# Linear attention's products in 64x64 quarters of TensorE, ahead of a mixture of experts

## The chip, the core and the metric

The kernel runs on one core of one Trainium2 chip. The metric is the device time of one execution in microseconds (us). A core has a matrix engine (TensorE, PE in the profile), a vector engine (VectorE, DVE), an activation engine (ScalarE, ACT), a general engine (GpSimd, POOL) and a queue engine (SyncE, SP). DMA transfers bring data from memory; here they are issued mostly by POOL and SP. TensorE multiplies a stationary block, loaded by a weight load (PEld), with a stream of columns, and writes to PSUM, from where VectorE and ScalarE read.

## What is computed

```python
def phi(x): return np.where(x > 0, x, np.exp(x) - 1.0) + 1.0
q_p, k_p = phi(q), phi(k)                      # (8, 8, 576, 64): batch, head, token, feature
kv  = np.einsum('bhsd,bhse->bhde', k_p, v)
z   = np.sum(k_p, axis=2)
num = np.einsum('bhsd,bhde->bhse', q_p, kv)
den = np.einsum('bhsd,bhd->bhs', q_p, z)[..., None] + 1e-06
x   = (num / den).transpose(0, 2, 1, 3).reshape(4608, 512)
P   = np.exp(x @ w_gate - max)                 # 8 experts
for _ in range(8):                             # sinkhorn: rows, then columns
    P /= P.sum(1, keepdims=True) + 1e-09
    P /= P.sum(0, keepdims=True) + 1e-09
    P *= 4608 / 8
out = sum(P[:, e:e+1] * (np.maximum(x @ w1[e], 0) @ w2[e]) for e in range(8))   # w1 512x1024, w2 1024x512
```

## The kernel before, in words

The program has two parts. The **front** is the attention of 16 items (8 batches times 2 groups of four heads), and it fills the tile xT with x, features on partitions, in fp16. The rest is the experts: layer 1 (x times w1, relu), layer 2 (times w2, scaled by P and added up), in blocks of 512 tokens, most of them by a scheme that multiplies 7 blocks in place of 8 (block7 and unit). While the front runs, the first blocks of expert 0 are worked off between its steps (hq at line 684, ye at line 932), so that TensorE has something to do.

**The order.** Every step is recorded in a planner (class _Plan) as a task with an engine, an assumed duration, a priority, and the buffers that it takes and uses. For the front the order is not planned: the string _FRONT lists task numbers with a letter for the engine (p TensorE, a ScalarE, d VectorE, g GpSimd, s SyncE, m a DMA, n none), and run() issues them just so. Once the list is used up, the planner picks by its assumed times and priorities. It also has a constant TURN, 0.13, that it adds on TensorE when a task's field cfg differs from that of the task ahead; before, cfg=1 marks only the kv task.

**One item,** in att(b, g), has four heads in two pairs; hh (0, 1) is the head inside a pair, which is also the half of the 128 partitions (64 partitions with 9 tokens each), and r (0, 1) is the pair:
- k (fp32), q and v (cast to fp16) are loaded by a DMA each (line 380). v goes into two of three blocks of a tile vv whose middle block holds ones.
- exp(k) on ScalarE (L390), max(k+1, 1) on VectorE (L394) and the minimum of both (L398) give phi(k), tile t. q goes the same way (L447, L450, L454), tile tq.
- f_kv (L413): 9 token steps times 2 halves hh, contraction over 64 partitions. The stationary block is 64x128, the heads of both pairs side by side, and the streamed one is v0, ones, v1: 192 columns. Of the result only the blocks that belong together are wanted.
- f_z (L340 on ScalarE, L342 on VectorE): two copies of 64 partitions by 256 columns put kv and z into the tile kvz, in which the off-diagonal blocks stay zero. Those zeros are set once by two memsets on GpSimd ahead of all loads (L604).
- f_qt (L439): 9 transposes of 128x128 turn phi(q), one copy (L342 or L340) brings it to SBUF, tile qpT.
- heads (L470): with the 128x128 block of kvz as stationary, two matmuls of 288 columns each give den (tile att) or num (tile num_ps) for half the tokens. So there are four such groups an item: den and num for each half.
- ScalarE takes the logarithm of den (L483) and exp of its negative (L488); VectorE multiplies num with that into xT (L498).

The zeros in kvz let one 128-row matmul do two heads at once, and half of its products are with zeros. After every second batch nine token blocks of logits are computed (L515, 36 matmuls of 8 columns), and after the last the sinkhorn loop starts (lines 541 to 565, its column sums by a matmul at L556). 46 warm-up matmuls (L590) fill TensorE's time at the start.

The order of the 512 features of x within xT is free as long as w1 (load_w1, L315) and the router weights (f_wg, L585) are loaded in the same order.

Of the kernel before, what the change touches and what calls it, by code (L numbers as in the profile page):

```python
# [11 lines left out]
FP16 = mybir.dt.float16  # L12
# [5 lines left out]
class _Plan:  # L18
# [121 lines left out]
    48s 49m 1n 2p 3p 52g 53m 4p 50g 51m 5p 6p 78g 79m 7p 8p 76g 77m 9p 10p 126g 127m 54a 55d 11p 12p 80g 81m 13p 14p  # L140
    128g 129m 56d 108n 109g 110m 57n 58p 0g 15p 130g 131m 16p 17p 18p 19p 20p 21p 61n 62a 63d 154g 155m 22p 23p 24p 25p
    26p 59a 64d 27p 111g 112m 60a 28p 29p 89n 90a 30p 91d 65p 31p 66d 32p 82a 156g 157m 33p 83d 67p 34p 68a 84d 158g
    159m 132a 69p 92d 35p 36p 133d 85n 86p 114g 115m 70a 71a 93p 87d 116g 117m 37p 88d 38p 94d 139n 140a 72p 39p 73d
    95p 40p 182g 183m 96a 134d 74p 75d 97p 41p 98a 184g 185m 141d 135n 136p 142d 99a 42p 143p 161d 186g 187m 137a 43p
    138a 144d 44p 160a 102p 210g 211m 145p 103d 113n 602p 146a 45p 162d 46p 47p 100p 119n 167n 120g 168a 169d 121m 603p
    101d 147p 148a 170d 163n 164p 212g 213m 149a 171p 165d 604p 214g 215m 166a 172d 152p 153d 173p 605p 174a 240g 241m
    555d 118n 606p 150p 601n 607a 175p 151d 608p 176a 610p 242g 243m 609d 188a 612p 189d 614p 244g 245m 195n 196a 190d
    616p 197d 613a 611d 191n 123g 192p 124m 615a 198d 618p 193a 194a 106g 217d 107m 177a 180p 199p 617d 216a 620p 181d
    200d 178p 619a 270g 271m 179d 621a 201p 122n 624p 202a 223n 225d 268g 269m 224a 639p 218d 203p 562d 638n 640a 219n
    220p 300g 301m 204a 226d 622p 205a 221d 298g 299m 222d 227p 247d 206p 228a 641p 207d 104g 105m 643p 253n 255d 246a  # L150
    642d 272g 273m 229p 644d 208p 230a 645p 209d 254a 231p 248d 647p 232a 256d 326g 327m 249n 250p 233a 646d 302g 303m
    257p 251d 125n 623p 252a 258d 281n 282a 236p 283d 259p 237d 625p 260a 284d 234p 632a 649p 235d 274a 261p 275d 628p
    262a 276d 354g 355m 629p 648a 311n 313d 563g 263a 285p 266p 286d 651p 304a 328g 329m 267d 238p 330g 331m 650a 630d
    356g 357m 277n 278p 305d 239a 306d 626p 279a 280a 333d 312a 264p 287p 265d 627p 288a 384g 385m 652d 307n 308p 332a
    314d 440g 441m 289p 309d 634a 653p 382g 383m 636d 290a 310d 358g 359m 672p 556d 291a 334d 315p 292p 654a 316d 659p
    339n 340a 293d 317p 657p 361d 318a 360a 341d 294p 660p 295d 319p 557d 412g 413m 671n 673d 335n 336p 320a 558s 559m
    442g 443m 342d 658p 337a 321a 338d 343p 667d 322p 367n 368a 344d 674p 323d 296p 388a 362d 324p 297a 369d 655p 675a
    325d 414g 415m 665a 345p 395n 397d 656p 386g 387m 346a 370d 416g 417m 396a 676p 389d 564d 347p 418a 390d 363n 364p
    565s 566m 567s 568m 348a 661p 365d 444g 445m 398d 677a 371p 349a 366d 662p 372d 663a 352p 373p 353d 678p 374a 425n
    427d 350p 679a 375p 351d 680p 376a 419d 426a 391n 392p 420d 669a 399p 500g 501m 428d 377a 688p 576g 393d 400d 682p  # L160
    394a 446a 681d 380p 401p 381d 690p 402a 498g 499m 447d 683a 378p 684p 379d 496g 497m 403p 577d 685d 421n 422p 404a
    448d 429p 423a 472g 473m 424a 686p 430d 405a 583g 406p 687d 705p 453n 454a 407d 431p 691p 455d 432a 468g 469m 510n
    512d 511a 408p 584g 433p 409d 707p 434a 698d 470g 471m 449n 450p 704n 708a 456d 505g 706d 689p 451a 435a 513d 457p
    709p 696a 458d 452a 502a 692p 578d 475d 579s 580m 438p 560s 561m 459p 439d 694p 460a 581s 582m 436p 461p 437d 711p
    462a 481n 483d 464p 463a 503d 410p 693p 465d 411a 712a 504d 482a 514p 466p 695p 467d 474a 710d 506n 507p 515a 484d
    713p 476d 508a 509a 715p 741d 714a 702d 516p 742d 477n 478p 517a 569d 716a 518p 727p 479d 519a 570g 480a 485p 520a
    521p 486d 717p 522d 487p 719p 718d 488a 571d 523p 720a 489p 700d 572s 573m 746p 490a 574s 575m 524d 748p 491a 743d
    494p 721p 745n 747a 495d 749a 728p 744d 585d 492p 750p 493d 752p 553n 784d 751a 785d 525p 753a 737d 754p 786d 526a
    787s 788m 528d 756p 586s 587m 755a 789s 790m 735a 722p 757a 738d 554p 588s 589m 729a 527n 529p 723p 739d 530d 1015s
    1016m 724p 740d 531d 758p 760p 759a 725p 761a 762d 792p 532p 794p 793a 590g 533d 597n 598g 599m 726p 763d 795a 731a  # L170
    591n 592g 593m 796p 764d 733a 798p 534d 842g 800p 799a 766p 802p 767a 806p 791n 797a 768p 801d 807a 803d 535p 770p
    536d 843d 808p 537d 844g 812p 809a 772p 813a 771a 814p 773a 816p 804p 769a 817d 776p 845s 846m 805a 765d 1072s
    1073m 810p 777d 818p 815d 774p 819a 900d 811a 850p 538p 820d 901g 778p 851a 775d 856p 779a 539d 864p 857a 594g 595m
    902d 866p 821d 854p 824p 540d 849n 855a 860p 825a 826p 865a 867a 852p 870p 822d 853a 872p 871a 861d 830p 873d 874p
    831a 868p 875d 862p 596n 1007d 834p 863a 823d 827a 876p 1008d 869a 541p 858p 835d 908p 958g 832p 859d 909a 877a
    836p 833d 542d 912p 837a 878d 910p 922p 959d 911a 879d 914p 828p 543d 915a 882p 907n 913a 829a 916p 923a 918p 883a
    924p 917d 928p 925a 1009d 884p 929a 919d 888p 880d 885a 960d 930p 889a 881d 961s 962m 544p 932p 903s 904m 926p 933d
    963s 964m 892p 927a 931d 920p 893d 905s 906m 934p 921a 545d 890p 546d 847s 848m 966p 968p 967a 886p 935a 969a 894p
    891d 547p 972p 936d 895a 980p 887a 937d 970p 940p 548d 965n 971a 549d 973a 942p 981a 941a 974p 976p 986p 975d 984p
    946p 977d 985a 943a 938d 550p 944p 947a 551d 987a 552d 982p 950p 983a 939d 637g 783a 990p 951d 978p 991d 988p 979a  # L180
    948p 1010d 1018p 949d 992p 1019a 989d 1020p 635a 952p 1024p 600n 1006n 1011d 1021a 1000p 953a 1025a 1026p 957g 631a
    1022p 1028p 993a 701g 998p 1017n 1029d 1023a 1027d 1001p 699g 1030p 1005d 1032p 1528n 1529g 1530m 1012d 1034p 1033a
    996p 1013d 898g 703a 999p 1035a 1038p 1004a 839g 1040p 1031a 1036p 1039a 997p 633g 1037a 1041d 1042p 1075p 1043d
    994p 1076a 1003d 1077p 1014d 1044p 1078a 945d 995p 1129s 1130m 1045a 1081p 1046d 1002a 1083p 1047d 1079p 1050p
    1048d 1049d 1052p 1051a 1082a 1055p 1054d 730d 1085p 1053d 1058a 1060p 1074n 1080a 1086d 1059g 668a 1063p 666g
    1061d 1084d 1087p 1062d 1089p 780g 1088a 1065d 1091p 1090a 1066p 1092a 664g 1056a 1095p 1068d 1097p 1064d 1096a
    896g 1093p 1067d 1099p 670d 1094a 1132p 840g 1134p 1133a 1100d 1069p 1135a 1098d 1101p 1070d 1138p 1071d 1102a
    1186s 1187m 1140p 1139a 1103d 1136p 1107p 1131n 1137a 1104d 1109p 1105d 1108a 736a 1106d 1112p 1111d 1110d 1142p
    1113a 1117p 1115a 1143d 1114g 1120p 1116g 1119d 897d 1144p 955g 1118d 1146p 1145a 1148p 1147a 1123p 841g 1149a
    1152p 1125d 1154p 1124d 1534n 1535g 1536m 1153a 1150p 1141d 732a 1156p 1057g 1189p 1151a 1157d 1191p 1190a 1121d  # L190
    1126p 1192a 1155d 697a 1158p 1122d 1195p 1128d 1159a 1243s 1244m 1127d 1197p 1196a 1160d 1193p 1164p 1161d 1166p
    1162d 1165a 781a 1169p 1168d 1188n 1194a 1167d 1199p 1163d 1174p 1200d 1177p 1175d 1176d 1201p 1198d 1203p 1205p
    1204a 1180p 1206a 1202a 1209p 1182d 1211p 1181d 1210a 1207p 1170a 1213p 1208a 1246p 1214d 1248p 1247a 1212d 1183p
    1249a 1178d 1172a 1215p 1185d 1252p 1184d 1216a 1300s 1301m 1254p 1217d 1250p 1221p 1179d 1245n 1251a 1218d 1223p
    1222a 1219d 1253a 1226p 1220d 734a 1224d 1256p 1227a 1225d 1231p 1257d 1228g 1234p 1171g 1232d 1255d 1258p 1173g
    1233d 1260p 782d 954g 1262p 1261a 1237p 1263a 1259a 1266p 1531g 1532m 1239d 1268p 1238d 1267a 1264p 1235d 838a
# [28 lines left out]
def kernel(  # L225
# [10 lines left out]
    nc = tc.nc  # L236
# [125 lines left out]
    def att(b, g):  # L362
# [70 lines left out]
        def qps():  # L433
            return (at2.rearrange("p a b -> p (a b)").bitcast(FP16)[:, 0:NJ * P]
                    .rearrange("p (j h w) -> p h j w", h=2, w=PW))
# [167 lines left out]
    for t in kvz_t:  # L603
        nc.gpsimd.memset(t, 0.0)  # L604
# [604 lines left out]
```

## Time and profile before

| what | us |
|---|---|
| median of 3 runs (964.11 to 965.62) | 964.44 |
| the profiled execution | 967.64 |
| its span in the trace | 965.6 |
| TensorE, VectorE, ScalarE, GpSimd busy | 950.3, 782.0, 579.3, 184.6 |
| the last multiply into xT ends | 118.9 |
| the last logits' exponential starts | 120.7 |

Busy times of TensorE count each matmul from its start to its modelled end, so that matmuls overlap; what one costs is the distance to the next start. In a timeline row stand the start, the duration of the merged group, the engine, the line, what it writes and reads, the array's tile (rows*columns) and the streamed shape, and the count; in brackets the idle time ahead and what ended it. "issue" means that the profile shows nothing that was waited for.

### The profile page before, as it was taken

The page shows a single profiled execution, that of the slowest core. Times are in us where ns is not written, and L with a number is a line of the kernel's source. Part 1 is how long each engine was busy: PE and PEld are TensorE (multiplying, and loading weights), DVE is VectorE, ACT ScalarE, POOL GpSimd, SP SyncE. Part 2 cuts the span into 40 slices and gives each one's busy share as a digit, 9 for nine tenths or more (in the row PEclk, how much of TensorE's full clock was granted, in tenths as well). Part 3 has the DMA queues.
Part 4 walks back from the last instruction along what each step waited for, and adds up shares of the span by engine and source line. Part 5 has one row for each costly group of instructions (what it writes and reads, how often), then busy time and mean ns, then how long its engine had stood idle before and what let it go on. Part 6 is the DMA issues. An engine that isn't in the chain of part 4 may idle for free.

```text
span 965.6 us, 21108 instructions
## 1 busy us (share of the span) xinstructions
PE 950.3 (98%) x8576; PEld 805.2 (83%) x8576; DVE 782.0 (81%) x1474; ACT 579.3 (60%) x1031; POOL 184.6 (19%) x238
## 2 busy tenths in 40 slices
PE   7999999999999999999999999999999999999998
PEld 4555568888888888888888888888888888888886
DVE  6899899778888788878887888878887888877775
ACT  6898856666655555555555555555555555555553
POOL 6435021452111121111112111111112111111110
PEclk9999999999999999999999999999999999999999
DMA  9999382225323352262226322272226322235654
GB/s 220 244 249 209 106 235 80 53 88 121 98 77 100 99 120 78 89 153 78 77 78 133 105 72 72 72 159 71 76 75 139 100 77 77 78 99 164 165 163 111
DMA packets 45681, 112.52 MB, mean 117 GB/s; under 512 B 4368, under 2 KB 25616, under 8 KB 45584
## 3 DMA queue, kind: packets, MB, share of 16 engines
q1 hardware_dynamic: 21056, 75.57, 24.0%
q0 software_dynamic: 24128, 35.07, 19.8%
q8 instruction: 67, 1.10, 0.5%
q10 hardware_dynamic: 400, 0.52, 0.2%
q14 instruction: 30, 0.25, 0.1%
HBM read 119.69 MB, written 17.69 MB: 142 GB/s over the span
## 4 chain that ended last, share of the span: by engine, by line
PE 95%; DMA 2%; DVE 2%; issue 0%; ACT 0%; POOL 0%; DVEq 0%; ACTq 0%; POOLq 0%
PE ye L1050 36%; PE hq L810 24%; PE R L810 12%; PE Zye L810 6%; PE Zye L1050 6%; PE ye L932 4%; PE hq L684 3%; DMA vv<-in_v_dram 2%; PE kv_ps L413 1%; PE att L439 1%; PE att L470 1%; PE num_ps L470 1%; DVE wt L549 0%; PE att L515 0%; PE yw L590 0%
## 5 line engine op out<-in xcount | busy, mean ns | idle before, releaser
L1081 DVE SCALAR_TENSOR_TENSOR acc<-ye,P_sb,acc 128x256 f32<-128x256 f32 x620 | 268.8, 479 | 124.7 <-PE ye L1050 123.1
L810 PEld LDWEIGHTS <-W 128*128 128x128 f16 x2144 | 209.9, 98 | 25.5
L1050 PEld LDWEIGHTS <-S 128*128 128x128 f16 x1984 | 194.1, 98 | 22.8 <-DVE S L1021 0.4
L1091 POOL TENSOR_TENSOR acc<-acc,st 128x256 f32<-128x256 f32 x124 | 88.1, 730 | 601.0 <-ACT st L1088 594.5
L1050 PE MATMUL ye<-T,S 128*128 128x256 f16 x1488 | 192.8, 273 | 0.1
L810 PEld LDWEIGHTS <-w 128*128 128x128 f16 x1608 | 157.5, 98 | 19.8 <-issue 1.1
L1050 PEld LDWEIGHTS <-h 128*128 128x128 f16 x1584 | 154.9, 98 | 18.0
L845 ACT ACTIVATE h<-hq 128x512 f16<-128x512 f32 x134 | 80.2, 598 | 130.6 <-PE hq L810 127.7
L810 PE MATMUL R<-xs,W 128*128 128x256 f16 x1008 | 151.2, 273 | 0.0
L810 PE MATMUL hq<-xs,W 128*128 128x256 f16 x1008 | 151.2, 273 | 0.0
L810 PE MATMUL hq<-xs,w 128*128 128x256 f16 x1008 | 140.9, 273 | 0.3 <-DVE h L848 0.3
L825 ACT COPY Zye<-hq 128x512 f32<-128x512 f32 x134 | 77.7, 580 | 47.6 <-PE hq L810 47.3
L842 ACT ACTIVATE h<-Zye 128x512 f16<-128x512 f32 x134 | 80.0, 597 | 43.0 <-PE Zye L810 42.7
L848 DVE CUSTOM_DVE_ANT_0 h<-R,s 128x512 f16<-128x512 f32 x126 | 86.5, 686 | 13.0 <-ACT s L832 13.0
L1021 DVE TENSOR_TENSOR S<-h 128x1024 f16<-128x1024 f16 x124 | 86.1, 694 | 11.2 <-ACT h L845 11.2
L1088 ACT ACTIVATE st<-Zye,P_sb 128x256 f32<-128x256 f32 x124 | 53.1, 471 | 69.1 <-PE Zye L1050 68.2
L832 ACT COPY s<-hq 128x512 f32<-128x512 f32 x126 | 73.5, 583 | 32.3 <-PE hq L810 31.8
L848 DVE CUSTOM_DVE_ANT_0 h<-hq,s 128x512 f16<-128x512 f32 x126 | 86.6, 687 | 5.1 <-PE hq L810 2.6
L810 PE MATMUL Zye<-xs,w 128*128 128x256 f16 x504 | 75.6, 273 | 0.0
L839 ACT COPY s<-R 128x512 f32<-128x512 f32 x126 | 74.6, 592 | 1.2 <-PE R L810 0.7
L1050 PE MATMUL ye<-w,h 128*128 128x256 f16 x528 | 68.4, 273 | 0.0
L1050 PE MATMUL Zye<-w,h 128*128 128x256 f16 x528 | 68.4, 272 | 0.0
(125 smaller groups left out, 1013.8 us busy)
## 6 DMA issues: line engine op xcount, KB each, us to landing
xs<-xd SPq DMA_DIRECT2D x63, 896.0 KB, 4.6
kin<-in_k_dram POOLq DMA_DIRECT2D x15, 576.0 KB, 8.3
out_dram<-acc SPq DMA_DIRECT2D x67, 128.0 KB, 2.4
w<-in_moe_w_dram POOLq DMA_DIRECT2D x16, 512.0 KB, 7.7
w<-in_moe_w_dram POOLq DMA_DIRECT2D x7, 1024.0 KB, 13.1
vv<-in_v_dram POOLq DMA_DIRECT2D x16, 288.0 KB, 9.0
qin<-in_q_dram POOLq DMA_DIRECT2D x16, 288.0 KB, 7.6
xd<-acc SPq DMA_DIRECT2D x5, 512.0 KB, 3.6
```

The lines of the kernel that those rows point to most:

```text
L810: nc.tensor.matmul(dst[:, p, :], lhsT=lhs(p, c), rhs=rhs(c), start=(first and p == 0 and c == 0), stop=(c == 1), skip_group_check=True)
L825: nc.scalar.copy(out=Zt[1], in_=gX["tile"])
L832: nc.scalar.copy(out=gs2["tile"], in_=gX["tile"])
L839: nc.scalar.copy(out=gs5["tile"], in_=gR["tile"])
L842: nc.scalar.activation(out=hd(0, 0), in_=Zt[1], func=AF.Relu)
L845: nc.scalar.activation(out=hd(1, 0), in_=gX["tile"], func=AF.Relu)
L848: nc.vector._custom_dve(TENSOR_ADD_SAT, out=dst, in0=ps, in1=sb, s0=3.0e38, s1=0.0)
L1021: nc.vector.tensor_tensor(out=Sx[:, i], in0=a0, in1=a1, op=op)
L1050: nc.tensor.matmul(bank(g_)[:, s, :], lhsT=lhs(s, kk), rhs=rhs(kk), start=(new and s == 0 and kk == 0), stop=(kk == 3), skip_group_check=True)
L1081: nc.vector.scalar_tensor_tensor(out=dst(), in0=bank(g_)[:, s, :], scalar=P_sb[:, gg, e:e + 1], in1=dst(), op0=ALU.mult, op1=ALU.add)
L1088: nc.scalar.mul(out=gst["tile"], in_=bank(g_)[:, s, :], mul=P_sb[:, gg, e:e + 1])
L1091: nc.gpsimd.tensor_tensor(out=dst(), in0=dst(), in1=gst["tile"], op=ALU.add)
```

## The change

Every product of the attention goes to TensorE in 64x64 quarters, addressed by the partitions of the operands (rows) and of the result (columns).
- kv: 4 matmuls a token step in place of 2, each one head's 64x64 block of phi(k) against 128 columns (its v and the ones). The result is dense, all heads' kv and z.
- kvz loses the zero blocks: half the size, no memsets, and one copy of 128 partitions by 256 columns in place of two of 64.
- The turning of phi(q): 36 transposes of 64x64 in place of 9 of 128x128, with the two halves hh in different banks of PSUM.
- den and num: 4 matmuls a group in place of 2, contraction over 64 partitions.
- The heads now land in another order of the features of x, and w1 and the router are loaded in that order, with 128 partitions in each transfer.
- All these tasks have cfg=1 and other assumed times, and the string _FRONT is another one, with other task numbers. In it the first load of POOL is q in place of v, and the four loads of the first half-size pieces of w1 stand behind the fourth v.

```diff
-    kvz_t = [fp.tile([P, 2, 2, P], FP16, ...) for i in range(2)]
+    kvz_t = [fp.tile([P, 2, 2, D], FP16, ...) for i in range(2)]
...
-        return load_w(moe_w1, "w1", p_w1, [[((slice(64 * r, 64 * r + 64),), 256 * F * r, [[F, PW], [PW * F, NDT], [1, F]])
-                                            for r in range(2)]], e, shape=[P, NDT, F], **kw)
+        return load_w(moe_w1, "w1", p_w1, [[((slice(None), slice(2 * i, 2 * i + 2)), P * i * F,
+                                             [[F, P], [256 * F, 2], [1, F]]) for i in range(2)]], e, shape=[P, NDT, F], **kw)
...
-                    nc.tensor.matmul(gkv["tile"][:, hh, 0:3 * D].rearrange("p (r d) -> p r d", r=3),
-                                     lhsT=gt["tile"][s, j, :, :].rearrange("p r d -> p (r d)"), rhs=gin["v"]["tile"][s, :, j, :],
-                                     start=(j == 0), stop=(j == NJ - 1))
+                    for r in range(2):
+                        nc.tensor.matmul(gkv["tile"][64 * r:64 * r + 64, hh, 0:2 * D].rearrange("p (z d) -> p z d", z=2),
+                                         lhsT=gt["tile"][s, j, r, :], rhs=gin["v"]["tile"][s, r:r + 2, j, :],
+                                         start=(j == 0), stop=(j == NJ - 1))
...
-        for r in range(2):
-            def f_z(e, r=r):
-                s = slice(64 * r, 64 * r + 64)
-                src = gkv["tile"][s, :, 64 * r:64 * r + 2 * D].rearrange("p h (z d) -> p h z d", z=2)
-                dst = gz["tile"][s, :, :, 64 * r:64 * r + 64]
-                copy(e, dst, src if r == 0 else src[:, :, ::-1])
-            tz.append(fadd({"dve": 0.43, "act": 0.37}, f_z, deps=[tkv, *tz], use=[gkv, gz], prio=pr))
+        def f_z(e):
+            copy(e, gz["tile"].rearrange("p h z d -> p h (z d)"), gkv["tile"][:, :, 0:2 * D])
+        tz = [fadd({"dve": 0.43, "act": 0.4}, f_z, deps=[tkv], use=[gkv, gz], prio=pr)]
...
             for j in range(NJ):
-                nc.tensor.transpose(at2...[:, P * j:P * j + P], gtq["tile"][:, j].rearrange("p r d -> p (r d)"), ident)
+                for hh in range(2):
+                    s = slice(64 * hh, 64 * hh + 64)
+                    for r in range(2):
+                        nc.tensor.transpose(qps()[64 * r:64 * r + 64, hh, j, :], gtq["tile"][s, j, r, :], ident[s, s])
...
         def heads(dst, c, z):
-            for hh in range(2):
-                nc.tensor.matmul(dst[:, hh, 0:CH], lhsT=gz["tile"][:, hh, z, :],
-                                 rhs=gq["tile"][:, hh, :, :].rearrange("p j w -> p (j w)")[:, CH * c:CH * c + CH],
-                                 start=True, stop=True)
+            for r in range(2):
+                s = slice(64 * r, 64 * r + 64)
+                for hh in range(2):
+                    nc.tensor.matmul(dst[64 * hh:64 * hh + 64, r, 0:CH], lhsT=gz["tile"][s, hh, z ^ r, :],
+                                     rhs=gq["tile"][s, hh, :, :].rearrange("p j w -> p (j w)")[:, CH * c:CH * c + CH],
+                                     start=True, stop=True)
...
-    for t in kvz_t:
-        nc.gpsimd.memset(t, 0.0)
```

More of the change, by code (lines that the diff above doesn't have):

```diff
@@ L145 @@
[L145 to L154, printed above, removed]
@@ L288 @@
     vv_t = [fp.tile([P, 3, NJ, D], FP16, tag=f"vv{i}", name=f"vv{i}", bufs=1) for i in range(NV)]
-    kvz_t = [fp.tile([P, 2, 2, P], FP16, tag=f"kvz{i}", name=f"kvz{i}", bufs=1) for i in range(2)]
+    kvz_t = [fp.tile([P, 2, 2, D], FP16, tag=f"kvz{i}", name=f"kvz{i}", bufs=1) for i in range(2)]
     kvps = front.enter_context(tc.tile_pool(name="kvps", bufs=1, space=PSUM))
@@ L463, in att @@
         tm = fadd(("dve", 0.76), f_qp, deps=[t2, t3], use=[geq, gtq], prio=pr)
-        t1 = fadd(("pe", 0.52), f_qt, deps=[tm, t_id[0]], acq=ga, use=[gtq], prio=pr)
+        t1 = fadd(("pe", 0.5), f_qt, deps=[tm, t_id[0]], acq=ga, use=[gtq], prio=pr, cfg=1)
         tq = fadd({"act": 1.13, "dve": 0.76}, f_qc, deps=[t1], acq=[gq], use=[*ga, gq], prio=pr)
@@ L584, in f_wg @@
     def f_wg(_, r):
-        nc.gpsimd.dma_start(out=wg_sb[64 * r:64 * r + 64], in_=AP(tensor=moe_w_gate.tensor, offset=256 * E * r,
-                                                                  ap=[[E, PW], [E * PW, NDT], [1, E]]))
+        nc.gpsimd.dma_start(out=wg_sb[:, 2 * r:2 * r + 2], in_=AP(tensor=moe_w_gate.tensor, offset=P * E * r,
+                                                                  ap=[[E, P], [256 * E, 2], [1, E]]))
     t_id[0] = add(("pool", 0.6), f_init, prio=-290.0, after=1.75)
```

168 lines of the change are left out of this document (88 added, 80 removed).

## The prediction

> **What bounds the kernel now.** I read the page first, for the share of each engine and the chain that ended last, and then the table by stretches.
>
> ```profile
> PE 950.3 (98%) x8576; PEld 805.2 (83%) x8576; DVE 782.0 (81%) x1474; ACT 579.3 (60%) x1031; POOL 184.6 (19%) x238
> PE 95%; DMA 2%; DVE 2%; issue 0%; ACT 0%; POOL 0%; DVEq 0%; ACTq 0%; POOLq 0%
> ```
> ```profile
> 0.00:30.00 30.00, 23.30 (x182) 12.23 (x183) 19.24 (x33) 19.69 (x23) 17.52 (x30) 1.00 1.05 220
> 30.00:119.00 89.00, 86.61 (x782) 50.58 (x781) 83.30 (x135) 79.32 (x109) 32.33 (x41) 1.00 0.90 205
> 119.00:126.00 7.00, 7.00 (x67) 3.87 (x66) 6.75 (x17) 3.58 (x7) 0.43 (x2) 1.00 0.60 215
> 126.00:135.00 9.00, 7.05 (x36) 3.88 (x34) 8.66 (x16) 3.47 (x7) 3.52 (x4) 0.81 1.10 242
> 135.00:200.00 65.00, 65.00 (x571) 55.32 (x569) 53.98 (x108) 41.84 (x77) 17.40 (x13) 1.00 0.37 98
> ```
>
> The second line of the first fence says that TensorE ends the chain almost everywhere. In the table the columns are PE, weight loads, VectorE, ScalarE and GpSimd, then the granted clock. Attention lies in the first two stretches. In the second TensorE idles 2.4 us of 89, but VectorE is busy 83.3 and ScalarE 79.3: three engines are full together, and TensorE is full partly because the front order slips expert 0's products between attention's. So a TensorE microsecond saved there is worth up to a microsecond, as long as the other two can hand it more work. Behind attention nothing changes: in the built programs the last 966 VectorE, 667 ScalarE and 6,972 TensorE matmul instructions stand in the same order. The whole question is how much earlier the front is through.
>
> **TensorE, part by part.** The timeline of one attention item, TensorE only (start, duration):
>
> ```profile
> 75.95 0.41 PE L470 MATMUL att<-qpT,kvz 128*128 128x288 f16 x2
> 76.29 0.92 PE L413 MATMUL kv_ps<-vv,t 64*128 64x192 f16 x18
> 77.14 1.04 PE L932 MATMUL ye<-w,h 128*128 128x512 f16 x4
> 78.01 0.67 PE L439 MATMUL att<-ident,tq 128*128 128x128 f16 x9
> 78.52 1.03 PE L932 MATMUL ye<-w,h 128*128 128x512 f16 x4
> 79.38 0.41 PE L470 MATMUL num_ps<-qpT,kvz 128*128 128x288 f16 x2
> 79.62 0.41 PE L470 MATMUL att<-qpT,kvz 128*128 128x288 f16 x2
> 79.87 1.03 PE L684 MATMUL hq<-xT,w 128*128 128x512 f16 x4
> ```
>
> Durations overlap, so a price is the distance from one start to the next. Turning phi(q): 78.52 - 78.01 = 0.51 us for nine matmuls. Two groups of heads: 79.87 - 79.38 = 0.49, so 0.245 a group and 0.1225 a matmul. The kv group is already in half-height tiles (64 rows). Its first 100 ns, in stretches of 10 ns (PE column: matmuls in flight; then loads):
>
> ```profile
> 76.29:76.30 0.01, 0.01 (x2) 0.01 (x2) 1.00 0.00 0
> 76.30:76.31 0.01, 0.01 (x2) 0.01 (x4) 1.00 0.00 0
> ...
> 76.37:76.38 0.01, 0.01 (x2) 0.01 (x4) 1.00 0.67 115
> 76.38:76.39 0.01, 0.01 (x4) 0.01 (x6) 1.00 0.00 0
> ...
> 76.46:76.47 0.01, 0.01 (x5) 0.01 (x3) 1.00 0.00 0
> 76.47:76.48 0.01, 0.01 (x6) 0.01 (x4) 1.00 1.33 230
> ```
>
> Two matmuls begin together, the next two some 0.083 us later: 192 columns at about 0.43 ns each, as in the heads (122.5 ns / 288). So the two row halves really work side by side, and a kv group streams for 9 x 0.083 = 0.75 us. It also pays for the change of tile shape: the head matmul before it should have released TensorE at 75.95 + 0.245 = 76.195, kv starts at 76.29 (0.095 later), and ye starts at 77.14 where 76.29 + 0.75 = 77.04 was possible (0.10 later). A run of tiled work costs 0.195 beside its own time.
>
> Before, by item: heads 4 x 0.245, kv 0.75, turning 0.51, one run 0.195. Sixteen items: 15.7 + 12.0 + 8.2 + 3.1 = 39.0 us.
>
> After, everything here is in 64x64 quarters, four at a time:
> - Heads, four matmuls of 288 columns a group: 0.125 if the four overlap, 0.245 if only row halves do. I take 0.125, by the pair above: 64 x 0.125 = 8.0.
> - kv, 36 matmuls of 128 columns (the third block of columns is no longer computed). Nine rounds of 128 columns at 0.43 ns give 0.50; a load and a matmul every 25 ns (below) give 0.90. I take 0.50: 8.0.
> - Turning, 36 of 64 columns: nine rounds by columns 0.25, at 25 ns each 0.90. No row shows a round shorter than the present transpose, so I take that nearest row, 0.51: 8.2.
> - Tile changes: the built order of the changed TensorE program has 56 unbroken runs of tiled groups where the old one has 16. 56 x 0.195 = 10.9; with only the 0.095 on entry seen as sure, 5.3.
>
> Sum 35.1, so **-3.9 us**. Most of what the heads give is paid back at the tile changes. The products of expert 0 placed ahead of the last logits are 248 matmuls where 252 stood, so the front is not shortened by pushing work out of it.
>
> **The other engines.** Two kv copies of 64 partitions become one of 128 with the same 256 columns:
>
> ```profile
> L340 ACT CAST kvz<-kv_ps x19: 348/367/371, 10.3 to 110.8; 64x256 f16<-64x256 f32 x19
> L342 DVE CAST kvz<-kv_ps x13: 406/417/428, 16.7 to 110.0; 64x256 f16<-64x256 f32 x13
> ```
>
> The price goes by columns here, so I keep 0.367 and 0.417 (bounds: half to double). The new order has 9 on ScalarE and 7 on VectorE: 10 x 0.367 = 3.7 and 6 x 0.417 = 2.5 us less. This lets VectorE, 94% busy in the second stretch, follow TensorE most of the way. The reversal of the second copy costs nothing extra either way.
>
> The zeroing of the kv tiles goes, and it stands ahead of the first loads on GpSimd:
>
> ```profile
> 0.72 0.99 POOL L604 MEMSET kvz<- 128x512 f16 x2 [0.29 <-POOLq L1193]
> 1.65 0.87 POOL L380 DMA_DIRECT2D vv<-in_v_dram  x1
> ```
> ```profile
> 9.26 1.16 ACT L447 ACTIVATE eq<-qin 128x1152 f16<-128x1152 f16 x1 [3.45 <-DMA qin<-in_q_dram]
> ...
> 27.73 0.92 PE L413 MATMUL kv_ps<-vv,t 64*128 64x192 f16 x18 [1.58 <-DMA vv<-in_v_dram]
> ```
>
> All GpSimd loads can start 0.93 us sooner, and the front's beginning waits for them. In the new order all four parts of w1 stand behind the fourth v load, where two stood ahead of it; the 1.58 us wait for that load should shrink too. I count **-0.9** for the start and **-1.0** for the wait (bounds 0 and -1.6), because copies and exponentials (20 of 30 us busy) take part of it. With less shelter at the start, the first w1 product is late next; it stands after 46 warm-up matmuls in both orders. The w1 and router loads keep their bytes but go to 128 partitions; I count 0, since those warm-ups and three items' products lie ahead of w1's first use. Were that cover gone, the first product would wait as kv does above, 1.58. The new order of x features changes only which rows of w1 and the router meet which rows of x: 0.
>
> **Sum:** -3.9 - 0.9 - 1.0 = -5.8. The profiled execution took 967.64 us, 2.04 around its span of 965.6, and lies 3.2 above the median of 964.44. The differences apply to either: profiled near 961.8, median near **958.5** (own range 955 to 962).
>
> **Rivals.** *Issue instead of columns (slower).* The smallest distance shown is in the logits:
>
> ```profile
> 71.97 1.04 PE L515 MATMUL att<-wg_sb,xT 128*128 128x8 f16 x36
> 72.87 0.41 PE L470 MATMUL num_ps<-qpT,kvz 128*128 128x288 f16 x2
> ```
>
> 36 load and matmul pairs in 0.90 us, 25 ns each at 8 columns. If quarters cannot go faster, kv and turning cost 0.90 each: 16 x (0.40 + 0.39) = +12.6, giving 971. It breaks even where 1,152 pairs fill the 39.0 - 8.0 - 10.9 = 20.1 us left to them: 17.4 ns a pair, with the 1.9 of the start on top 19.1. For it: no row shows 14 ns. Against it: in the 10 ns table two matmuls and four loads are under way 20 ns after kv begins. The Trainium skill, "TensorE: Matmul & The Clock Gate", Part 1, gives the same floor of about 25 ns, and its Part 3 about 4 ns between different tiles; this trace has a row like each.
>
> *Weight loads in turn (much slower).* A load of 128 columns lasts 98 ns here:
>
> ```profile
> L1050 PEld LDWEIGHTS <-S 128*128 128x128 f16 x1984 | 194.1, 98 | 22.8 <-DVE S L1021 0.4
> ```
>
> Half the columns is 49 ns; 36 one after another are 1.76 us, and 32 groups add 32 x (1.76 - 0.505) = 40: 998. The overlapping loads of kv speak against it for the row halves; nothing shows column halves. The Trainium skill, "TensorEngine Tiling (Array Packing)", Restrictions, says that column tiling disables Fast Weight Load; that rule would be this rival's cause, and with loads side by side it costs nothing beyond my 0.51.
>
> *VectorE becomes the bound (no change).* Its work falls by 2.5 only; if its waits for TensorE at the tile changes eat the earlier start and part of that, 0.5 to 2 us remain: 962.5 to 964.
>
> *A stall behind the front goes (faster still).* In the sinkhorn stage one VectorE row lasts 3.16 us beside GpSimd work, TensorE waits, and the clock of the stretch falls to 0.81:
>
> ```profile
> 120.74 0.23 ACT L519 ACTIVATE P_sb<-att 128x72 f32<-128x72 f32 x1 [0.28 <-PE att L515]
> ...
> 122.12 0.68 DVE L549 TENSOR_TENSOR wt<-P_sb,Rr 128x288 f32<-128x288 f32 x1
> ...
> 126.88 3.16 DVE L549 TENSOR_TENSOR wt<-P_sb,Rr 128x288 f32<-128x288 f32 x1
> ...
> 127.25 1.17 POOL L726 TENSOR_TENSOR xst<-xT 128x512 f16<-128x512 f16 x1
> ...
> 130.58 0.39 PE L556 MATMUL R<-gs,ones_t 128*128 128x8 f32 x2 [1.95 <-DVE gs L551]
> ```
>
> 1.95 idle and 0.19 x 9 = 1.7 of clock. The new order puts more expert 0 work between the first two column sums, and GpSimd's x blocks elsewhere. If nothing collides: 958.5 - 3.6 = 955. It may as well collide again, so the forecast keeps it.
>
> **How the numbers follow.** Forecast 0.43, stall gone 0.18, VectorE bound 0.15, issue 0.20, loads in turn 0.04. A measurement tells about 0.2% (1.9 us). Faster: 0.43 + 0.18 = 0.61. Same: 0.12 of VectorE's 0.15. Slower: 0.03 + 0.20 + 0.04 = 0.27. The range 952 to 971 leaves out the loads in turn (0.04), half of the issue case (0.10) and the end of the fastest one (0.04).
>
> **What would show it.** Right: den and num groups 0.12 to 0.13 apart inside a run, kv and turning near 0.5, about 0.2 lost at each tile change, the last logits near 116 instead of 120.7. The first q landing near 7 us instead of 9.3 shows the start. Wrong: kv or turning above 0.61 us (17 ns a pair); tile changes above 0.26 us a run (3.9 / 56 more than I count); or the last logits no earlier, with VectorE's waits on TensorE grown.

## The result, and the profile after

The changed kernel takes 963.59 us (median of 20 runs, 959.61 to 965.95), the kernel before 965.05 (20 runs, 963.67 to 969.88). The ratio is 0.9976, 95% interval [0.9965, 0.9987]: faster by 0.24%, or 2.3 us [1.3, 3.4]; the two medians alone differ by 1.5 us. The forecast was 958.5, a fall of 5.8 us by its sum, with an own range of 955 to 962: the direction came true, of the size less than half, and the median lies above that range. Below, microseconds of a ratio are (ratio - 1) x 965.

The profiled execution took 964.32 us with a span of 962.0, where before it was 967.64 and 965.6. Here are the same stretches as in the prediction, with the same columns (PE, weight loads, VectorE, ScalarE, GpSimd, granted clock, DMA share, GB/s):

```profile
0.00:30.00 30.00, 23.28 (x388) 10.47 (x388) 19.41 (x33) 20.34 (x22) 19.09 (x30) 0.93 1.06 234
30.00:119.00 89.00, 86.25 (x1466) 40.17 (x1466) 80.66 (x132) 73.67 (x100) 31.11 (x40) 0.96 0.89 211
...
126.00:135.00 9.00, 9.00 (x76) 7.15 (x75) 8.62 (x22) 5.24 (x10) 1.41 (x1) 1.00 0.12 40
...
25.00:30.00 5.00, 3.28 (x50) 1.25 (x49) 2.40 (x4) 1.97 (x2) 2.71 (x4) 0.61 1.17 206
30.00:40.00 10.00, 10.00 (x129) 4.20 (x129) 7.76 (x14) 7.27 (x10) 4.63 (x7) 0.86 1.18 264
60.00:70.00 10.00, 10.00 (x142) 3.89 (x131) 8.05 (x14) 7.69 (x11) 3.75 (x5) 0.83 0.65 142
```

Three things are to be seen. The clock, 1.00 in both front stretches before, is 0.93 and 0.96 now; the finer rows put the loss at 25 to 40 us and at 60 to 70. The stretch from 126 to 135, where the clock was 0.81, is whole again: the stall of the sinkhorn stage is gone. And in the long stretch TensorE is about as busy as before (86.25 us, 86.61 then), while VectorE and ScalarE have 2.6 and 5.7 us less to do.

One attention item of the changed kernel on TensorE (start, duration; x is the number of matmuls):

```profile
64.03 0.32 PE L472 MATMUL att<-qpT,kvz 64*64 64x288 f16 x4
64.28 1.04 PE L684 MATMUL hq<-xT,w 128*128 128x512 f16 x4
65.25 0.70 PE L415 MATMUL kv_ps<-vv,t 64*64 64x128 f16 x36
65.78 0.48 PE L440 MATMUL att<-ident,tq 64*64 64x64 f16 x36
66.19 1.04 PE L932 MATMUL ye<-w,h 128*128 128x512 f16 x4
67.16 0.32 PE L472 MATMUL num_ps<-qpT,kvz 64*64 64x288 f16 x4
67.31 0.29 PE L472 MATMUL att<-qpT,kvz 64*64 64x288 f16 x4
...
80.38 0.48 PE L440 MATMUL att<-ident,tq 64*64 64x64 f16 x36
80.68 0.30 PE L472 MATMUL num_ps<-qpT,kvz 64*64 64x288 f16 x4
```

From start to start: a group of heads 0.15 (67.31 - 67.16; others 0.14), kv 0.53 (65.78 - 65.25), turning 0.30 (80.68 - 80.38), 8.3 ns for each load and matmul. Four ye products take 0.87, so ye from 66.19 ends at 67.06 and the heads begin 0.10 later; turning and exit together take 0.41 (66.19 - 65.78), 0.11 for the exit. A tile change and its way back cost about 0.19 to 0.2, as forecast. By these starts the quarters cost 64 x 0.145 + 16 x 0.53 + 16 x 0.30 + 56 x 0.19 = 33.2 us where 39.0 stood: -5.8.

The other rows that matter, in order of time (in brackets the idle time before the row and who ended it):

```profile
1.22 0.87 POOL L381 DMA_DIRECT2D qin<-in_q_dram  x1 [0.80 <-POOLq L1193]
...
6.03 1.16 ACT L447 ACTIVATE eq<-qin 128x1152 f16<-128x1152 f16 x1 [4.03 <-DMA qin<-in_q_dram]
...
23.80 0.70 PE L415 MATMUL kv_ps<-vv,t 64*64 64x128 f16 x36 [0.51 <-DVE xT L500]
25.37 0.32 PE L472 MATMUL num_ps<-qpT,kvz 64*64 64x288 f16 x4 [0.87 <-DVE kvz L343]
...
27.34 2.72 PE L684 MATMUL hq<-xT,w 128*128 128x512 f16 x6 [1.35 <-DMA w<-in_moe_w_dram]
...
30.61 3.43 PE L684 MATMUL hq<-xT,w 128*128 128x512 f16 x10
...
42.17 2.15 DVE L454 TENSOR_TENSOR tq<-tq,eq 128x1152 f16<-128x1152 f16 x1
42.53 1.16 POOL L729 TENSOR_TENSOR acc<-xT,acc 128x512 f16<-128x512 f16 x1
44.37 0.48 PE L440 MATMUL att<-ident,tq 64*64 64x64 f16 x36 [1.26 <-DVE tq L454]
...
55.61 2.22 DVE L399 TENSOR_TENSOR t<-t,ek 128x1152 f16<-128x1152 f16 x1
56.04 1.17 POOL L729 TENSOR_TENSOR acc<-xT,acc 128x512 f16<-128x512 f16 x1
58.55 1.04 PE L517 MATMUL att<-wg_sb,xT 128*128 128x8 f16 x36 [1.31 <-DVE qpT L343]
```
```profile
L521 ACT ACTIVATE P_sb<-att x4: 218/230/231, 59.6 to 118.7; 128x72 f32<-128x72 f32 x4
```

The first q is there at 6.03 where it was at 9.26, also because it is now loaded first. GpSimd's first load starts at 1.22 instead of 1.65: 0.43 sooner and not 0.93, because GpSimd idles 0.80 ahead of it. From 23 us on TensorE waits for VectorE (0.51, 0.87) and the first product of w1 for its load (1.35). At the full clock such a product takes 0.216 us (four ye in 0.87); the 16 from 27.34 to 29.99 and from 30.61 to 33.98 take 6.0 us together in place of 3.5, of which the low clock has about 2.4. At 42 and at 56 us a VectorE row that otherwise lasts 0.75 lasts 2.15 and 2.22 beside a GpSimd add of x blocks, and TensorE waits. The last logits' exponential (second view, the four of them: first and last start) is at 118.7 in place of 120.7; about 116 was forecast.

### The profile page after: what moved, and what is told of

It is laid out like the page before. It is cut to its first block, busy times and chain, and to the rows that moved or that the text cites. A ratio compares the mean times of both kernels' runs of the same rounds, so it can differ in the third digit from the quotient of the medians.

```text
span 962.0 us, 22778 instructions
## 1 busy us (share of the span) xinstructions
PE 947.0 (98%) x9424; PEld 791.3 (82%) x9424; DVE 778.0 (81%) x1474; ACT 575.9 (60%) x1023; POOL 176.8 (18%) x228
## 4 chain that ended last, share of the span: by engine, by line
PE 93%; DMA 3%; ACT 2%; POOL 1%; DVE 1%; issue 0%; ACTq 0%; DVEq 0%; POOLq 0%
PE ye L1050 35%; PE hq L810 24%; PE R L810 12%; PE Zye L810 6%; PE Zye L1050 6%; PE ye L932 4%; PE hq L684 3%; DMA w<-in_moe_w_dram 2%; DMA qin<-in_q_dram 1%; POOL acc L900 1%; PE kv_ps L415 1%; PE num_ps L472 0%; PE att L472 0%; ACT rden L485 0%; PE att L440 0%; PE att L517 0%
```

## The experiments

The theories that the expectations speak of: **A**, the quarters save what the starts show, and the new front order gives most of it back through waits and the halved clock; **B**, VectorE and ScalarE bound the front; **C**, quarters count as too little activity, and that lowers the clock. Where an expectation speaks of 3.4 us for the 16 products of w1, it took the low clock for all of them; by the starts above it is about 2.4. All results, each against the kernel before on the same chip:

| run | code and order | median us | ratio, 95% interval | us |
|---|---|---|---|---|
| old_order_quarters | after, old order | 964.20 | 0.9987 [0.9975, 0.9999] | -1.3 |
| new_order_halves | before, new order | 968.16 | 1.0028 [1.0017, 1.0038] | +2.7 |
| no_pool_adds | after, x blocks on VectorE | 960.41 | 0.9950 [0.9936, 0.9965] | -4.8 |
| filler | after, 14 filler products | 959.69 | 0.9943 [0.9930, 0.9957] | -5.5 |
| early_w1 | no_pool_adds, w1 sooner | 960.86 | 0.9947 [0.9934, 0.9959] | -5.1 |
| before_no_pool_adds | before, x blocks on VectorE | 959.85 | 0.9939 [0.9927, 0.9951] | -5.9 |
| quarters_old_no_pool | after, old order, x blocks on VectorE | 957.22 | 0.9912 [0.9899, 0.9925] | -8.5 |
| quarters_new_clean | after, filler, x blocks on VectorE | 956.92 | 0.9909 [0.9896, 0.9922] | -8.8 |
| halves_new_clean | before, new order, both | 966.53 | 1.0017 [1.0007, 1.0026] | +1.6 |
| clean_turn_whole | clean, turning whole | 958.98 | 0.9927 [0.9914, 0.9941] | -7.0 |
| clean_kv_halves | clean, kv in halves | 964.09 | 0.9985 [0.9975, 0.9996] | -1.4 |
| clean_memsets | clean, memsets back | 958.64 | 0.9924 [0.9911, 0.9936] | -7.3 |
| clean_control | clean once more | 957.09 | 0.9916 [0.9903, 0.9929] | -8.1 |
| clean_early_second_load | clean, a load sooner | 955.59 | 0.9901 [0.9886, 0.9915] | -9.6 |
| early_second_load | after, that load sooner | 960.92 | 0.9957 [0.9942, 0.9972] | -4.1 |

### Code and order apart

The change has two halves that can be run alone: the tiling with the old order's sequence of tasks, and the new sequence with the old tiling.

```diff
 # old_order_quarters: the changed kernel
-_FRONT = """ (its own) """
+_FRONT = """ (the order of before, its task numbers mapped, second kvz copies left out) """
 # new_order_halves: the kernel before
-_FRONT = """ (its own) """
+_FRONT = """ (the order of after, a second kvz copy behind each first) """
```

> All products in quarters, but the front order of the kernel before (its task list carried over, the second kvz copy of each item dropped). Theory A (the quarters save about 5.8 us of TensorE by the distances in the changed trace, the new order gives about 4 back through three waits and two stretches of half clock): the old order has 61 runs of tiled groups instead of 56, so TensorE saves 4.9; there is no late w1 load, so no fall of the clock near 27 us; the zeroing of kvz ahead of the loads is gone as well: 959 to 961, clock near 1.00 to 120 us. Theory B (VectorE and ScalarE bound the front, the gain of the changed kernel is the stall behind the front that went): 964 to 965, with more idle time of TensorE in the front. Theory C (quarters count as too little activity, and the clock falls wherever they stand alone): the clock falls in this front too, 964 to 967.

> The kernel before with the front order of the changed one (each item's second kvz copy directly behind the first, on the same engine). Theory A: the three waits of the new order (1.35, 1.26, 1.31 us) and the half clock behind two of them come with it, and nothing is saved on TensorE: 968 to 971, clock below 0.9 between 25 and 40 us. Theory B: the order is what gained the 1.5 us, so 963 to 965. Theory C: no quarters, so no fall of the clock anywhere in the front, 965 to 967.

The old order with quarters gained only 1.3, not the 4 to 6 that A expected; 964.20 is what B forecast. Its timeline, with GpSimd, shows why it has no more:

```profile
79.03 3.49 DVE L452 TENSOR_TENSOR tq<-tq,eq 128x1152 f16<-128x1152 f16 x1
79.62 1.17 POOL L724 TENSOR_TENSOR acc<-xT 128x512 f16<-128x512 f16 x1
80.74 1.15 POOL L725 TENSOR_TENSOR acc<-xT 128x512 f16<-128x512 f16 x1
82.91 0.32 PE L470 MATMUL num_ps<-qpT,kvz 64*64 64x288 f16 x4 [2.20 <-DVE kvz L341]
...
88.69 0.69 DVE L689 TENSOR_SCALAR h<-hq 128x512 f16<-128x512 f32 x1
89.05 1.15 POOL L725 TENSOR_TENSOR acc<-xT 128x512 f16<-128x512 f16 x1
89.30 0.75 DVE L498 TENSOR_TENSOR xT<-num_ps,rden 128x576 f16<-128x576 f32 x1
```
```profile
80.00:90.00 10.00, 7.11 (x116) 3.11 (x113) 9.78 (x14) 5.86 (x8) 6.10 (x7) 1.00 0.90 184
```

Beside two adds the VectorE row takes 3.49 us, and TensorE stands for 2.20. Rows that read PSUM (h, and xT from num_ps) keep their 0.69 and 0.75 beside the same adds. The Trainium skill, "GPSIMD Engine Reference", 1. Specifications, says that GpSimd shares its SBUF interfaces with VectorE and contends with VectorE instructions that have two SBUF inputs or run in a two-port mode; the held rows here are of these kinds, the rows from PSUM are not, so the trace agrees, and adds the size: about 1.4 us for each 1.15 us add.

In the same stretch TensorE idles 2.9 of 10 us, with quarters, and the clock stays 1.00. The new order with the old tiling, in contrast, has the fall without any quarter:

```profile
25.00:30.00 5.00, 2.81 (x30) 1.98 (x30) 3.80 (x8) 4.94 (x6) 2.14 (x3) 0.85 1.16 206
```

So in these profiled executions quarters are not needed for the fall, and waits beside quarters are not enough for it: C, as it stands, fails by both. Other executions of old_order_quarters have mean clocks down to 0.994 (the profiled one 0.999), so it is not free of falls either; what decides is worked out further down.

### The two losses taken away one at a time

```diff
 # no_pool_adds: the changed kernel, ten blocks of x differences from GpSimd to VectorE
-    ... 540g ... 547g ... 548g ... 562g ... 555g ... 568g ... 769g ... 828g ... 885g ... 886g ...
+    ... 540d ... 547d ... 548d ... 562d ... 555d ... 568d ... 769d ... 828d ... 885d ... 886d ...
 # filler: the changed kernel, 14 warm-up products more: one warm-up task where it stood, with 3 of them,
 # four set later, ahead of the TensorE tasks 98, 161, 149 and 586, with 2, 3, 4 and 7
-    def f_warm(_):
-        nc.tensor.matmul(yw[0], lhsT=warm[:, 0:P], rhs=warm, start=True, stop=True)
+    def f_warm(_, n=1):
+        for _i in range(n):
+            nc.tensor.matmul(yw[0], lhsT=warm[:, 0:P], rhs=warm, start=True, stop=True)
```

> The changed kernel, but the ten fp16 adds of the x blocks that the front order gives to GpSimd run on VectorE at the same places. Theory A: the two VectorE rows of 2.15 and 2.22 us near 42 and 56 us last 0.75 again, TensorE's waits of 1.26 and 1.31 us go, and with the second the half clock at 60 to 64 us (worth 1.7); VectorE has about seven adds of 0.42 more in the front, 2.9, some of it in its idle time: 960 to 962. Theory B: VectorE is the bound, so its 2.9 us more are added in full and its 2.9 us of stretching go, 963 to 964. Theory C: the clock falls as before, 963 to 965.

> The changed kernel with 14 more warm-up matmuls of 512 columns, placed where TensorE waits between 22 and 27 us (3 ahead of the fourth kv, 4 ahead of the next num, 7 ahead of the first w1 product). Theory A: the clock stays at 1.00 between 25 and 33 us, the 16 w1 products that took 0.43 us each take 0.216, which saves up to 3.4 us there, less about 1 for filler that stands in the way: 960.5 to 962.5. Theory B: the earlier products only wait for VectorE later on, 963 to 965. Theory C: the filler raises the clock near 27 us, but the fall near 60 us stays: 961 to 963.

Against the changed kernel's 0.9976, the first is worth 2.5 us and the second 3.2, each within about 1.7 by the intervals. Filler's 959.69 lies below A's range. Without the adds the row of 42 us has its 0.75 again, in the timeline of that kernel:

```profile
42.07 0.75 DVE L453 TENSOR_TENSOR tq<-tq,eq 128x1152 f16<-128x1152 f16 x1
```

and its clock is 1.00 from 40 on, but still low at 25 to 40. With the filler it is the other way round; timeline and stretches of that kernel:

```profile
26.95 1.68 PE L592 MATMUL yw<-warm 128*128 128x512 f16 x7
28.47 1.46 PE L685 MATMUL hq<-xT,w 128*128 128x512 f16 x6
```
```profile
25.00:30.00 5.00, 5.00 (x97) 2.48 (x89) 3.25 (x6) 2.64 (x3) 2.32 (x3) 1.00 1.16 207
...
50.00:60.00 10.00, 8.70 (x148) 4.28 (x146) 8.47 (x13) 6.70 (x10) 4.42 (x6) 0.84 1.14 265
```

TensorE, given work that has no use, keeps its clock there, and six products of w1 take 1.46 instead of 2.72; the second fall only moves, to between 50 and 60 us. Is it the late load of w1 alone?

```diff
 # early_w1: no_pool_adds, and the first two loads of w1 ahead of the third and fourth v
-    ... 128g ... 155g ... 106n 107g 108m ... 109g 110m ...
+    ... 106n 107g 108m 128g ... 109g 110m 155g ...
```

> The changed kernel without adds on GpSimd and without more warm-ups, but the first two loads of w1 are issued ahead of the third and the fourth v. If the fall of the clock near 27 us came from TensorE's waits that end in the late w1 load: no fall, 957 to 958.5, as with the filler. If other waits of that stretch were enough (kv then waits for the v loads that went behind): the clock falls as in the kernel without GpSimd adds, 960 to 961.5.

It is not: the time is that of no_pool_adds, and in the timeline the wait of w1 is gone, others stand in its place, and the six products are slow all the same:

```profile
24.91 0.32 PE L471 MATMUL num_ps<-qpT,kvz 64*64 64x288 f16 x4 [1.88 <-DVE xT L499]
26.65 1.17 PE L414 MATMUL kv_ps<-vv,t 64*64 64x128 f16 x36 [1.06 <-DVE tq L449]
...
29.22 2.74 PE L683 MATMUL hq<-xT,w 128*128 128x512 f16 x6
```

### The clean comparison

Now the x blocks on VectorE in both orders, and the filler in the new one (in the front of the old one the clock of the profiled executions stayed 1.00).

```diff
 # before_no_pool_adds: the kernel before, its nine blocks (13 adds)
-    ... 563g ... 576g ... 583g ... 584g ... 570g ... 842g ... 844g ... 901g ... 958g ...
+    ... 563d ... 576d ... 583d ... 584d ... 570d ... 842d ... 844d ... 901d ... 958d ...
 # here, in early_w1 and in all clean versions the planner no longer has GpSimd to choose for these tasks;
 # the traces of before and after have no such add beyond those of the lists
-            last = add({"dve": 0.756, "pool": 3.1} if i == 0 else {"dve": 0.42, "pool": 1.55}, f_T,
+            last = add({"dve": 0.756} if i == 0 else {"dve": 0.42}, f_T,
 # quarters_old_no_pool: old_order_quarters with the same
 # quarters_new_clean: no_pool_adds and filler together
 # halves_new_clean: new_order_halves with both
```

> The kernel before, all fp16 adds of the x blocks on VectorE instead of GpSimd, at the same places. Theory A (the quarters are worth about 5 us of TensorE, and what hid it are VectorE rows held up beside GpSimd adds and stretches of half clock): the three rows of 2.0, 2.8 (two together) and 3.16 us shrink, TensorE's waits near 95 and 130 us and the half clock behind the second go, 4 to 5 us, less some of 13 adds of 0.42 more on VectorE: 961 to 963. Theory B (VectorE bounds the front): its 5.5 us more work cancel the 6 it no longer loses, 965.

> Quarters in the old front order, no adds on GpSimd. Theory A: 4.8 us less TensorE time than the kernel before without GpSimd adds (61 runs of tiled work), and no zeroing ahead of the loads: 3.5 to 5.5 us below that kernel, 956 to 959. Theory B: the same as that kernel within 1.5 us.

> The changed kernel with both mendings: 14 more warm-up matmuls where TensorE waits between 22 and 27 us, and no adds on GpSimd. Theory A: the two gains were about 4 (filler) and 3 (adds) and meet different waits, so they add up: 956 to 957.5, and the clock stays at 1.00 through the front. Theory B: VectorE, with its added work, takes back the second: 959 to 960.

> The old products in the new front order with both mendings. Theory A: 5 to 6 us above the changed kernel with both mendings: 961 to 963. Theory B: no more than 1.5 us above it.

The single most effective edit of this study has nothing to do with the change: nine letters in the order, 13 adds, give the kernel before 5.9 us, more than A's range. In its timeline the row of 3.16 us from the prediction has its own length:

```profile
123.27 0.66 DVE L549 TENSOR_TENSOR wt<-P_sb,Rr 128x288 f32<-128x288 f32 x1
```

Quarters then add 2.6 in the old order, where A had expected 3.5 to 5.5. There TensorE idles 3.8 us between 20 and 115 us, by its waits mostly for VectorE and ScalarE, and 1.5 in before_no_pool_adds: B has a part. In the new order they add 10.4 (1.0017 to 0.9909), where A had expected 5 to 6, and without the two mendings 5.0 (1.0028 to 0.9976). The filler is not what keeps the halves back: their first product of w1 starts at 30.26 with it, and at 30.33 in new_order_halves. The last logits show the same, first in quarters_new_clean, then in halves_new_clean:

```profile
L520 ACT ACTIVATE P_sb<-att x4: 221/231/232, 55.1 to 112.4; 128x72 f32<-128x72 f32 x4
```
```profile
L520 ACT ACTIVATE P_sb<-att x4: 218/232/278, 59.2 to 120.9; 128x72 f32<-128x72 f32 x4
```

The order fits the faster tasks: it costs the halves 7.5 us (0.9939 to 1.0017) and the quarters nothing (0.9912 to 0.9909), with the filler in the new order alone.

### The parts, undone one at a time in the clean version

```diff
 # clean_turn_whole
-                for hh in range(2):
-                    s = slice(64 * hh, 64 * hh + 64)
-                    for r in range(2):
-                        nc.tensor.transpose(qps()[64 * r:64 * r + 64, hh, j, :], gtq["tile"][s, j, r, :], ident[s, s])
+                nc.tensor.transpose(at2...[:, P * j:P * j + P], gtq["tile"][:, j].rearrange("p r d -> p (r d)"), ident)
 # clean_kv_halves: lhsT of 64x128, 192 columns, and two copies of 64 partitions
-                    for r in range(2):
-                        nc.tensor.matmul(gkv["tile"][64 * r:64 * r + 64, hh, 0:2 * D]...
+                    nc.tensor.matmul(gkv["tile"][:, hh, 0:3 * D].rearrange("p (r d) -> p r d", r=3),
 # clean_memsets: four memsets of the kvz tiles ahead of GpSimd's first load
+    for t in kvz_t * 2:
+        nc.gpsimd.memset(t, 0.0)
```

> The changed kernel with both mendings (14 more warm-up matmuls, no adds on GpSimd; call it the mended kernel, 956.9), but phi(q) is turned by 9 transposes of 128x128 again. Theory A (TensorE is the bound there): 0.51 us in place of 0.30 an item, 16 times, 2.5 to 3.5 us more: 959.5 to 960.5. Theory B (the turning is hidden): 957.

> The mended kernel, but kv in half-height tiles of 64x128 with 192 columns again, and two copies of 64 partitions in each kvz task. Theory A: 0.75 in place of 0.53 us an item (3.5), perhaps a second change of tile shape beside the quarters (up to 2), and 16 copies more on VectorE and ScalarE, half of it felt at most: 960.5 to 963. Theory B: only the copies are felt, 957 to 959.

> The mended kernel with the zeroing of kvz (four memsets, about 1 us) ahead of the first GpSimd load again; nothing reads the zeros. Prediction's step: all loads start some 0.9 us later and the front begins later by that: 957.5 to 958. If the first load is not what the front waits for: 957.

Against 0.9909 they cost 1.8, 7.4 and 1.5 us, together 10.7, about as much as quarters and the missing memsets are worth in this order. The same clean version, run once more (clean_control, 0.9916), makes them 1.1, 6.7 and 0.8; the first and the third are not clear of the intervals, and the first lies below the 2.5 to 3.5 that A forecast, the second above A's range of 960.5 to 963. The heads, the fourth part, were not undone alone. That they bring about nothing is argued from the remainder and from the starts: they save 15.7 - 9.3 = 6.4, and the tile changes cost 10.6 - 3.1 = 7.5 more. The timeline of quarters_new_clean, kv and turning, and then that of clean_kv_halves:

```profile
65.48 0.70 PE L414 MATMUL kv_ps<-vv,t 64*64 64x128 f16 x36
66.00 0.48 PE L439 MATMUL att<-ident,tq 64*64 64x64 f16 x36
```
```profile
62.09 0.92 PE L413 MATMUL kv_ps<-vv,t 64*128 64x192 f16 x18
62.94 0.48 PE L440 MATMUL att<-ident,tq 64*64 64x64 f16 x36
```

From kv to the turning 0.85 instead of 0.52, 16 x 0.33 = 5.3; that the other 1.4 to 2 us come from the 16 copies more is argued from their 0.37 and 0.42 us each, not shown apart.

### A load behind attention

Every kernel with the new order so far, and none with the old one, has one wait of TensorE over 1 us between 200 and 300 us. It starts from a load of expert weights that GpSimd issues behind four scalings of acc. I put it ahead of them, in the clean version (with a control on the same chip) and in the changed kernel.

```diff
-    ... 1100g 1104p 718g ... 764g ... 716g ... 822g ... 1515g 1516m ...
+    ... 1100g 1104p 1515g 1516m 718g ... 764g ... 716g ... 822g ...
```

> The clean version once more, unchanged, on the same chip as the run with the earlier load, so that a difference of 1.2 us can be told: 956.9, ratio 0.991, TensorE idle by 1.5 us between 200 and 300.

> Clean version (quarters, new order, 14 products as filler, x blocks on VectorE), with one load of expert weights issued on GpSimd ahead of four scalings of acc in place of behind them, about 6.5 us sooner. Theory (part of the new order's own price lies behind attention, in a load that is issued too late: VectorE waits 2.2 us for it and TensorE 1.5 us for VectorE at 217 to 219 us): both waits go and the time falls by 1.2 to 1.5 us, to 955.4 to 955.7 or a ratio near 0.9895; the 100 us from 200 on show TensorE idle by 0.1 or less in place of 1.5. Rival (the wait is caught up again by slack behind it, or the scalings that come later make acc late): within 0.4 us of 956.9.

> The changed kernel as it is, with the same one load issued ahead of the four scalings. Theory: the 1.2 us that TensorE waits for VectorE at 224 us goes, and the time falls by 1.2 to about 962.4, ratio 0.9964 where the changed kernel has 0.9976. Rival: no difference.

The control's timeline, then its stretch from 200 to 300, and the same stretch with the load sooner:

```profile
202.88 4.64 POOL L901 TENSOR_SCALAR acc<-acc,P_sb 128x512 f32<-128x512 f32 x3
...
209.71 0.77 POOL L315 DMA_DIRECT2D w<-in_moe_w_dram  x1
...
216.84 0.69 DVE L983 TENSOR_TENSOR W<-w 128x1024 f16<-128x1024 f16 x1 [1.83 <-DMA w<-in_moe_w_dram]
```
```profile
200.00:300.00 100.00, 98.86 (x906) 88.44 (x905) 81.32 (x156) 58.80 (x111) 21.08 (x24) 1.00 0.40 105
```
```profile
200.00:300.00 100.00, 100.00 (x919) 89.61 (x917) 82.51 (x158) 59.27 (x112) 21.08 (x24) 1.00 0.40 107
```

TensorE idles 1.14 in the control and not at all with the load issued 6.6 us sooner; the medians are 957.09 and 955.59, with ranges (956.66 to 957.82, 955.40 to 956.27) that don't meet: 1.5 us. In the changed kernel it gave 1.8 (0.9976 to 0.9957), within intervals that overlap. With 955.59 us this is the fastest version found, faster than both kernels.

## Why the prediction was right or wrong

- **TensorE, -3.9: the mechanism right, the size larger (-5.8 by starts).** The turning was mis-sized: 0.51 was taken from the nearest row, 0.30 was measured. Heads came at 0.145 instead of 0.125, kv at 0.53 instead of 0.50, the tile changes at the forecast 0.19. That the tile changes eat most of what the heads give held; they eat all of it.
- **The rivals on TensorE are out.** Issue at 25 ns a pair: the turning has 8.3 ns, kv 14.7. Loads in turn: kv and turning would take 1.76. The floor of about 25 ns that the prediction gave from the Trainium skill, "TensorE: Matmul & The Clock Gate", Part 1, does not hold for quarters in these rows.
- **The start, -0.9: the size may be right, the step was not.** The first load starts 0.43 sooner and not 0.93. clean_memsets puts the price of the memsets at 0.8 to 1.5, and its interval takes in 0.
- **The wait for v, -1.0: the wait of 1.58 is gone, the time is not.** Waits for VectorE and for w1 took its place: TensorE is busy 23.28 us of the first 30, where it was 23.30.
- **The step that failed: "The w1 and router loads ... I count 0, since those warm-ups and three items' products lie ahead of w1's first use."** The cover was there as a count of products and not as time. They were through before w1 and the first items' VectorE work were there: 0.51 + 0.87 + 1.35 = 2.7 us of waits between 23 and 28 us, and half the clock from 26 us on. The prediction priced the lost cover at 1.58, one wait, and had no term for the clock of the front; the filler, which fills these waits with products of no use, gains 3.2. early_w1 shows that the late load alone is not the cause, and the trace agrees: the clock falls at 26.06, when the wait for w1 (25.99 to 27.34) has only begun.
- **The collisions with GpSimd were weighed at one place only.** "It may as well collide again, so the forecast keeps it": in the sinkhorn stage it did not, which by the prediction's own price is 3.6 us gained. But two new ones stand at 42 and 56 us, and no_pool_adds gives back 2.5 for them. That the forecast's direction came true is luck so far: without the gain in the sinkhorn stage, which the forecast had set aside, the changed kernel would by that price have been 3.6 - 2.3 = 1.3 us slower.
- **"Behind attention nothing changes"** was read from VectorE, ScalarE and TensorE; GpSimd's order of issues was not looked at. It costs some 1.5 (clean_early_second_load).
- **VectorE as the bound** is true in part of the old order with quarters (with its 61 runs 39.0 - 34.2 = 4.8 us by starts, of which 2.6 arrive) and not of the new one when its waits are gone.

Together: -5.8 - 1.5 - 3.6 + 3.2 + 2.5 + 1.5 = -3.7, where -2.3 [-3.4, -1.3] was measured. The rest of 1.4 is not settled; each of the terms is itself uncertain by one to two microseconds.

What lets the clock fall can be read from the traces. The stretch ahead of the first fall in the changed kernel and that at half clock:

```profile
22.70:26.00 3.30, 1.66 (x83) 1.27 (x79) 2.68 (x6) 3.07 (x4) 1.20 (x2) 1.00 1.10 214
26.10:32.80 6.70, 5.46 (x20) 1.73 (x21) 3.50 (x6) 1.91 (x2) 4.06 (x5) 0.50 1.21 207
```

In every one of the 17 traces the changes of the granted clock lie on a grid of 3.41 us: here it falls at 26.06, rises at 32.88, falls at 60.19 and rises at 63.60. Count in each interval of that grid the time in which columns stream through TensorE, 0.42 ns a column (0.216 us / 512; twice that at half clock), products side by side once. Of the intervals that begin within the first 950 us, the 12 at whose end the clock falls hold 0.26 to 1.28 us, and the 4,686 after which it stays 1.00 hold 1.31 or more. The changed kernel has 1.10 from 22.64 to 26.06 and 0.97 from 56.77 to 60.19; old_order_quarters, with its wait of 2.20, just 1.31 from 79.22 to 82.63, and keeps its clock. So the waits and the short products of an interval count together, and not one wait. The bound was found from these traces after the fact, and no run was made to test it.

It should also depend on where the grid lies, which differs between executions (the first rise of the 17 traces lies between 4.1 and 6.6 us): the 20 executions of the changed kernel have mean clocks from 0.994 (963.88 to 965.13 us) to 1.000 (960.06 us). The Trainium skill, "TensorE: Matmul & The Clock Gate", Part 1, ties the fall to an idle window of about 3.4 us. The length agrees with the grid. But the intervals ahead of these falls were not idle, and the longest wait beside them in the changed kernel is 1.35 us.

## What to carry to other kernels

Count cover in time, not in instructions: when the work that hides a load becomes faster, the cover shrinks with it, and a TensorE that then waits can lose more by its clock than by the wait. What counted for the clock here was the share of streaming in stretches of 3.41 us. A change of tiling and a change of order should be run apart and together, since each may be worth little without the other (2.6 and 10.4 us here), and a list of who shares time with GpSimd's adds belongs to every new order. When an order written by hand moves, read the queues that issue loads as well as the engines that compute.

## What the runs showed of the hardware

- 36 transposes of 64x64 in the four quarters take 0.30 us, 8.3 ns each with its weight load; 36 matmuls of 128 columns 0.53 (14.7 ns each).
- Entering and leaving quarter tiles costs 0.10 and about 0.1 us. A single group of heads between whole-array products (0.25, and 0.10 on entry) is dearer than the whole-array group that it replaces (0.245); the 0.25 holds its exit.
- A GpSimd add of 128x512 f16 (1.15 us) held the VectorE rows shown, of two SBUF operands, by about 1.4 us (0.75 to 2.15, 2.22, with two adds 3.49; 0.66 to 3.16 with two); the rows shown that read PSUM are not held. Nine such blocks, 13 adds, cost the kernel before 5.9 us.
- The granted clock changes on a grid of 3.41 us. It fell to half after intervals with at most 1.28 us of streaming columns, and stayed after all with 1.31 or more; in the changed kernel it fell with no wait above 1.35 us, and in old_order_quarters it stayed with 2.9 us of idle time in 10.
